# The first two tiles of an MLP: tile 1's first layer ahead of tile 0's second, both as seven products of quarters

## The chip, the cores and the metric

The kernel runs on one core of one Trainium2 chip. The metric is the device time of one execution in microseconds (us). A core has five engines that each work through their own list of instructions in order and wait for each other by semaphores: TensorE (PE in the profile; its weight loads are PEld), VectorE (DVE), ScalarE (ACT), GpSimd (POOL) and SyncE (SP). POOL and SP also issue the DMA transfers, POOL those that turn fp32 in memory into fp16 on the chip.

## The reference

An attention without softmax for 8 batches of 8 heads, 576 rows and a head width of 64, then an MLP over all 4608 rows:

```python
kv = np.einsum('bhsd,bhse->bhde', k, v)
out = np.einsum('bhsd,bhde->bhse', q, kv)
rms = np.sqrt(np.mean(out * out, axis=-1, keepdims=True) + 1e-06)
attn = out / rms * g_norm
x = attn.transpose(0, 2, 1, 3).reshape(4608, 512)
h = x @ w_in                       # 512 x 2048
g = h * (1.0 / (1.0 + np.exp(-1.702 * h)))
result = g @ w_out                 # 2048 x 512
```

## The kernel before

**Tiles.** There are nine tiles of 512 rows for the MLP: tile t < 8 holds the first 512 rows of batch t, tile 8 the last 64 rows (the `rest`) of all eight batches. Each tile has a first layer (x by w_in, gate, result gT) and a second (gT by w_out, result osb, stored to memory). A batch's attention has, for each of four pairs of heads: `q` (transposes on TensorE, copy qT on VectorE; batches 0 and 1 only), `kv` (products of k and v; copies to kvb or kvd), `out` (product with q; square on ScalarE), `ss` (sum of squares on TensorE; inverse root `rs` on ScalarE) and `apply` (VectorE writes x). From batch 2 on q is turned by DMA, the product comes out by rows (`rows`, `add_up`, `roots`, `turn`), and x is turned by DMA. Batch t+1's attention is spread over tile t.

**Products of quarters.** From tile 2 on a layer is not computed as 64 products of 512 columns but, after Strassen and Winograd, from quarters of its two matrices: seven products of quarters, 16 matrix products of 256 columns each, 112 in all. They need sums of quarters, which VectorE forms: of w_in (`w_in_sum`, ws), of w_out (`weight_sum`, tw), of x (`Sums`, xS) and of gT (`Seven.sums`, gS). In a first layer (`SevenIn`, L482) the columns are cut into four parts; a step such as "12" of a `Plan` is product 2 of part 1, four matrix products; banks of PSUM are copied in between and added (L480, L544, L546). In a second layer (`Seven`, L558) the products run in `ORDER`; `keep` copies a bank to SBUF on ScalarE, `place` adds or copies into osb. Tile 1 already runs its second layer so; both layers of tile 0 and tile 1's first are plain products (L422, L760).

**Order.** No scheduler moves anything: each engine runs its instructions as the Python code emits them. `dense` (L725) emits a tile; the dictionaries u1 and u2 hang other work behind a column, a step or a product: `at1(12, ...)` runs behind column 12 of the first layer, `at2(36, ...)` behind product 36 of the second. For tile 0 that is:

```python
at1(12, of(1, "pack_q", c))
at2(9 + 3 * c, of(1, "q", c))
at2((36, 37, 46, 47)[c], of(1, "kv", c))
o = (41, 43, 52, 53)[c]
at2(o, of(1, "out", c))
```

So batch 1's attention lies in tile 0's second layer. g_norm is multiplied into x for batch 0 (`apply` with g_col, L339); for the others w_in itself is scaled (`scale_w_in`, L188), in tile 0's second layer, ahead of the `w_in_sum`.

**Loads.** POOL issues one software queue in the order of the code: batch 0's q, k, v by pairs, w_in, then w_out's first quarter, batch 1's q, and so on alternately (L879 to L889). An issue waits for the landing of the one eight back. SP issues the stores and the DMA transposes, also in one order.

**Buffers.** PSUM has eight banks in three pools: ps_a (3), ps_h (3), ps_o (2). Of SBUF, gT and gS have one buffer each, osb and the copies of `keep` (qf) two.

Of the kernel before, what the change touches and what calls it, by code (L numbers as in the profile page):

```python
# [12 lines left out]
P = 128  # L13
# [3 lines left out]
def kernel(  # L17
# [27 lines left out]
    GROUP = 6  # L45
# [19 lines left out]
    qbuf = const.tile([P, NPAIR * NJ * P], F16)  # L65
    kraw = const.tile([P, NPAIR, 2 * NJ * D], F16)
# [121 lines left out]
    def scale_w_in(ko, engine):  # L188
        w = w_in_sb[:, ko]
# [5 lines left out]
    class Attention:  # L195
# [140 lines left out]
        def apply(self, c):  # L336
            o, rs, n = self.o[c]
            if c < NPAIR and self.b == 0:
# [12 lines left out]
    class Early(Attention):  # L351
        KEEP = 2
# [12 lines left out]
    class First(Early):  # L365


        ss_pool = (ps_o, "o")
# [23 lines left out]
    class Second(Early):  # L392


        ss_pool = rest_pool = (ps_h, "hT")

# [161 lines left out]
    class Seven:  # L558
# [10 lines left out]
        def sums(self, i0, i1, which=(0, 1, 2, 3)):  # L569
# [49 lines left out]
        def place(self, name, mo, with_, i, j):  # L619
# [9 lines left out]
            if self.t == B:  # L629
# [53 lines left out]
    def hid_seven(t, hid, seven, units1):  # L683
# [10 lines left out]
        for n, step in enumerate(todo.steps):  # L694
# [12 lines left out]
            for i0, i1, which in todo.ready.get(n, ()):  # L707
                seven.sums(i0, i1, (which,))
# [7 lines left out]

        left = {n: [lambda x=x: late(x) for x in steps] for n, steps in todo.late.items()}
        end = lambda: seven.sums(HF - 2, HF, (0,))
# [6 lines left out]
    def dense(t, units1, units2, group, deep, hid=None):  # L725
        hid = hid or Hidden(t)
        gT = hid.gT
        seven = None if deep else Seven(t, gT)
        cols = range(FO) if deep else [f for i in range(HF) for f in (i, HF + i)]
        ready = {} if deep else {8: (0, 4), 13: (4, 6), 15: (6, 8, (0,))}  # L730
        if group and t:
            order = [(ko, fo) for part in ((0, 3, 1, 2), range(4, group)) for ko in (0, 1) for fo in part]
            order += [(ko, fo) for ko in range(2, KO) for fo in range(group)]
            for ko, i in order:
                pool = (ps_h, "hT") if i < 3 else (ps_a, "att") if i == 3 else (ps_o, "o")
                hid.mm(ko, cols[i], *pool)
            for i in range(group):
                hid.gate(cols[i])
        left = {}
        if t >= SEVEN:  # L740
            left = hid_seven(t, hid, seven, units1)
            cols = ()
        for i, fo in enumerate(cols):
            if i >= group:
                for ko in range(KO):
                    hid.mm(ko, fo)
                hid.gate(fo)
            for u in units1.get(i, ()):
                u()
            if i in ready:  # L750
                seven.sums(*ready[i])
# [289 lines left out]
```

## Time and profile before

| what | us |
|---|---|
| median of three runs | 263.76 (263.72 to 264.36) |
| the profiled execution, time | 263.92 |
| the profiled execution, span of its instructions | 262.1 |
| TensorE, busy in the span | 253.6 |
| VectorE | 185.1 |
| ScalarE | 173.6 |
| GpSimd | 43.7 |

The span runs from the first to the last instruction of the core; all places in time below are counted from its start. The granted TensorE clock was 0.996 of full speed over the span. A row of the profile reads: line of the kernel, engine, operation, what it writes `<-` what it reads, shape, `x` count, then total busy time and the mean of one in ns, then the idle time of that engine just ahead of it and what ended it. In a view by time a row starts with its start and its length in us, and several equal instructions are merged into one. In the chain that ended last, a row is a piece of the one path from the end of the kernel back to its start. The rows of DMA issues give how many, the KB of each as they land, and the median time from issue to landing.

### The profile page before, as it was taken

To read this page: it belongs to the slowest core of one execution; us is meant where nothing else is said; L and a number is where in the kernel's file an instruction comes from. 1 tells how busy PE (TensorE), PEld (TensorE's weight loads), DVE (VectorE), ACT (ScalarE), POOL (GpSimd) and SP (SyncE) were. 2 spreads that over 40 slices of the span, in tenths; PEclk is the share of its full clock that TensorE was granted. 3 is DMA by queue.
4 is the path that set the end of the run, shared out by engine and by line. 5 is a ranking of instruction groups with operands and counts; after the bars stand their busy time and mean duration, and the time that the engine had idled before them with its cause. 6 is when DMAs were issued, how large, how long until landed. Compare 5 with 4: busy or idle time off the path is not lost.

```text
span 262.1 us, 6210 instructions
## 1 busy us (share of the span) xinstructions
PE 253.6 (97%) x2556; PEld 204.3 (78%) x2556; DVE 185.1 (71%) x324; ACT 173.6 (66%) x308; POOL 43.7 (17%) x68
## 2 busy tenths in 40 slices
PE   6899999999999999999999999999999999999992
PEld 5434554447888988898889988998899888888882
DVE  1540378868768995899589958995899587567831
ACT  3459836776649963996489748974798469737810
POOL 8863242005005001400050005000000000000000
PEclk9999999999999999999999999999999999999998
DMA  7999999999989946996899769946600620021005
GB/s 173 197 199 205 205 203 177 217 206 130 163 180 172 221 58 160 117 240 83 145 154 196 102 157 150 237 54 154 165 0 8 156 83 0 3 100 63 0 3 160
DMA packets 59806, 35.32 MB, mean 135 GB/s; under 512 B 31554, under 2 KB 57154, under 8 KB 59650
## 3 DMA queue, kind: packets, MB, share of 16 engines
q0 software_dynamic: 28608, 18.17, 50.1%
q1 hardware_dynamic: 30768, 16.36, 27.1%
q8 instruction: 20, 0.33, 0.5%
q10 hardware_dynamic: 402, 0.39, 0.5%
q14 instruction: 8, 0.07, 0.1%
HBM read 36.70 MB, written 9.44 MB: 176 GB/s over the span
## 4 chain that ended last, share of the span: by engine, by line
PE 92%; DMA 4%; POOL 1%; DVE 0%; issue 0%; ACT 0%; ACTq 0%
PE o L648 37%; PE h L530 33%; PE hT L422 10%; PE o L760 5%; PE kvp L221 2%; DMA vbuf<-in_v_dram 2%; DMA qraw<-in_q_dram 2%; PE outR L281 2%; PE ss L329 1%; PE outT L254 0%; PE q L403 0%; PE outT L258 0%; POOL kraw L89 0%; ACT sq L272 0%; DVE osb L628 0%
## 5 line engine op out<-in xcount | busy, mean ns | idle before, releaser
L648 PEld LDWEIGHTS <-gS 128*128 128x128 f16 x512 | 49.8, 98 | 5.5
L510 ACT ACTIVATE gT<-h 128x512 f16<-128x512 f32 x84 | 46.2, 605 | 5.1 <-PE h L530 5.1
L530 PEld LDWEIGHTS <-ws 128*128 128x128 f16 x448 | 43.8, 98 | 5.1
L648 PE MATMUL o<-tw,gS 128*128 128x256 f16 x384 | 46.3, 273 | 0.0
L530 PE MATMUL h<-xS,ws 128*128 128x256 f16 x336 | 45.3, 273 | 0.0
L648 PEld LDWEIGHTS <-gT 128*128 128x128 f16 x384 | 37.1, 98 | 4.2
L530 PEld LDWEIGHTS <-w_in_sb 128*128 128x128 f16 x336 | 32.5, 98 | 3.9
L648 PE MATMUL o<-w_out_sb,gT 128*128 128x256 f16 x256 | 33.3, 273 | 0.0
L422 PE MATMUL hT<-xT,w_in_sb 128*128 128x512 f16 x128 | 28.9, 379 | 0.0
L625 DVE TENSOR_TENSOR osb<-o,qf 128x512 f32<-128x512 f32 (+1 forms) x25 | 16.7, 668 | 15.6 <-PE o L648 12.8
L530 PE MATMUL h<-xT,w_in_sb 128*128 128x256 f16 x192 | 27.1, 273 | 0.0
L89 POOL DMA_DIRECT2D kraw<-in_k_dram x11 | 8.1, 733 | 106.3 <-PE kvp L221 87.8
L580 DVE TENSOR_TENSOR gS<-gT 128x512 f16<-128x512 f16 (+2 forms) x34 | 22.0, 653 | 4.5 <-ACT gT L431 3.9
L544 DVE TENSOR_TENSOR h<-h,s 128x512 f32<-128x512 f32 x28 | 19.5, 698 | 7.4 <-PE h L530 5.6
L422 PEld LDWEIGHTS <-w_in_sb 128*128 128x128 f16 x128 | 12.3, 98 | 15.4 <-issue 0.9
L431 ACT ACTIVATE gT<-hT 128x512 f16<-128x512 f32 x32 | 17.6, 613 | 7.0 <-PE hT L422 7.0
L546 DVE TENSOR_TENSOR s<-h,s 128x512 f32<-128x512 f32 x28 | 19.4, 692 | 4.0 <-PE h L530 3.3
L331 ACT ACTIVATE rs<-ss,eps_t 128x512 f32<-128x512 f32 (+1 forms) x16 | 9.2, 584 | 16.4 <-PE ss L329 16.3
L510 ACT ACTIVATE gT<-s 128x512 f16<-128x512 f32 x28 | 17.3, 628 | 1.2 <-DVE s L546 1.2
L944 ACT ACT_TABLE_LOAD x14 | 18.0, 1283 | 0.3
L681 POOL DMA_DIRECT2D out_dram<-osb x2 | 1.1, 562 | 94.1 <-DVE osb L625 94.1
L760 PE MATMUL o<-w_out_sb,gT 128*128 128x512 f16 x64 | 16.7, 380 | 0.0
(93 smaller groups left out, 367.6 us busy)
## 6 DMA issues: line engine op xcount, KB each, us to landing
out_dram<-osb SPq DMA_DIRECT2D x10, 512.0 KB, 3.5
kraw<-in_k_dram POOLq DMA_DIRECT2D x6, 576.0 KB, 8.7
vbuf<-in_v_dram POOLq DMA_DIRECT2D x6, 576.0 KB, 12.1
qraw<-in_q_dram POOLq DMA_DIRECT2D x3, 512.0 KB, 13.3
qbuf<-in_q_dram POOLq DMA_DIRECT2D x3, 512.0 KB, 14.0
out_dram<-osb SPq DMA_DIRECT2D x6, 192.0 KB, 6.9
w_in_sb<-in_moe_w_in_dram POOLq DMA_DIRECT2D x4, 256.0 KB, 7.5
w_out_sb<-in_moe_w_out_dram POOLq DMA_DIRECT2D x2, 512.0 KB, 14.0
```

The source lines that it names most:

```text
L331: nc.scalar.activation(rs[:, 0:n], t[:, 0:n], AFT.Abs_reciprocal_sqrt, bias=eps_t, scale=1.0 / D)
L422: nc.tensor.matmul(self.h[fo], w_in_sb[:, ko, fo * P : (fo + 1) * P], self.x[:, ko], start=(ko == 0), stop=(ko == KO - 1),)
L431: nc.scalar.activation(self.gT[:, fo, :], self.h[fo], AFT.Gelu_apprx_sigmoid)
L510: nc.scalar.activation(self.gT[:, to, n * TH : (n + 1) * TH], src, AFT.Gelu_apprx_sigmoid)
L530: nc.tensor.matmul(bank[name][:, a], w, x, start=(p in (1, 5) and a == 0 and k == 0), stop=(k == KH - 1), skip_group_check=True,)
L544: nc.vector.tensor_add(bank["z"], bank["x"], self.s5)
L546: nc.vector.tensor_add(self.s5, bank["x"], self.s5)
L580: op(s[:, n, lo], a, b)
L625: nc.vector.tensor_add(o, ps, self.kept[with_][:, m])
L648: nc.tensor.matmul(o, a, w, start=(p in (1, 2, 5) and i == 0 and (mo == 0 or split)), stop=(i == HF - 1), skip_group_check=True,)
L760: nc.tensor.matmul(os[mo], gT[:, fo, mo * P : (mo + 1) * P], w_out_sb[:, fo, :], start=(fo == 0), stop=(fo == FO - 1),)
L944: u2.setdefault(i, []).append(lambda: f(*args))
```

## The change

The start of the kernel is put in another order: tile 0's first layer (still plain products, by columns), tile 1's first layer, tile 0's second, tile 1's second. Tile 1's first and tile 0's second layer become seven products of quarters. gT gets two buffers, gS stays one that tiles 0 and 1 share, and osb and qf go from two buffers to one.

- Batch 1's attention moves from tile 0's second layer into columns 8 to 15 of its first. Its k-v are kept pair by pair (`KEEP` 1) in two small copies each. Since ScalarE has its inverse-root table loaded for it, columns 12 to 15 are not gated at once: VectorE copies them into osb (free until then), and `gate_held` gates them within tile 1's first layer.
- Batch 1's x is scaled by g in `apply`, as batch 0's is. So w_in is scaled only behind both first layers: the four parts of w_in on ScalarE in tile 0's second layer, the four sums ws on GpSimd.
- All of batch 1's q, k, v are loaded ahead of w_out, in eight pieces ("q02" is q of pairs 0 and 1).
- The second layers of tiles 0 and 1 run in the order `FIRST`, and each half of their osb is stored as soon as it is there, in four pieces.
- The 64 `rest` rows of batch 0 move from tile 0 to tile 7; their q is kept in q_rest.

```diff
-    GROUP = 6
+    GROUP, HELD = 6, 12
...
-    gpool = ctx.enter_context(tc.tile_pool(name="gpool", bufs=1))
+    gpool = ctx.enter_context(tc.tile_pool(name="gpool", bufs=2))
     spool = ctx.enter_context(tc.tile_pool(name="spool", bufs=1))
-    opool = ctx.enter_context(tc.tile_pool(name="opool", bufs=2))
+    opool = ctx.enter_context(tc.tile_pool(name="opool", bufs=1))
...
-            rows = stage.tile([P, 6, 2 * P], F32, name="qf", tag="qf", bufs=2)
+            pool, tag, n1 = (opool, "osb", 8) if n == "v" else (stage, "qf", 6)
+            rows = pool.tile([P, n1, 2 * P], F32, name=tag, tag=tag, bufs=1)
...
-                self.kvp = ps_a.tile([P, NPAIR, D], F32, name="kvp", tag="att")
+                pool, tag = (ps_o, "o") if self.b < EARLY and c > 1 else (ps_a, "att")
+                self.kvp = pool.tile([P, NPAIR, D], F32, name="kvp", tag=tag)
...
-            if c < NPAIR and self.b == 0:
+            if c < NPAIR and self.b < EARLY:
...
-        KEEP = 2
+        KEEP = 1
+        ss_pool = (ps_o, "o")
...
+        def keep_rest(self):
+            for c in range(NPAIR):
+                nc.vector.tensor_copy(q_rest[:, c], self.qT[c][:, SM:S])
+        def rest(self, c):
+            return q_rest[:, c]
...
-            x = x if t < B else x.rearrange("p c (j r) -> p c j r", j=J)
+            x = x if EARLY <= t < B else x.rearrange("p c (j r) -> p c j r", j=J)
...
+        FIRST = (1, 2, 6, 5, 7, 3, 4)
-        def __init__(self, t, gT):
+        def __init__(self, t, gT, s=None):
             self.t, self.gT = t, gT
-            self.s = spool.tile([P, 4, HF, 2 * P], F16, name="gS", tag="gS")
+            self.s = s or spool.tile([P, 4, HF, 2 * P], F16, name="gS", tag="gS")
...
-                k = stage.tile([P, 6, HN], F32, name="qf", tag="qf", bufs=2)
+                k = stage.tile([P, 6, HN], F32, name="qf", tag="qf", bufs=1)
...
+            elif self.t < EARLY and j == 1 - i:
+                store_early(self.t, 2 * i * P, (2 * i + 2) * P)
...
-            for p in self.LAST if self.t == B else self.ORDER:
+            for p in self.FIRST if self.t < EARLY else self.LAST if self.t == B else self.ORDER:
...
+    def first_columns(hid, units):
+        for i in range(GROUP, FO):
+            for ko in range(KO):
+                hid.mm(ko, i)
+                if ko == 1:
+                    for u in units.get(i - 0.5, ()):
+                        u()
+            if i < HELD:
+                hid.gate(i)
+            else:
+                nc.vector.tensor_copy(osbs[0][:, i - HELD, :], hid.h[i])
+            for u in units.get(i, ()):
                 u()
...
+    def gate_held(hid, i):
+        nc.scalar.activation(hid.gT[:, i, :], osbs[0][:, i - HELD, :], AFT.Gelu_apprx_sigmoid)
+    sevens = {}
+    def first_layer(t, units, s=None):
+        hid = Hidden(t)
+        sevens[t] = Seven(t, hid.gT, s)
+        return hid_seven(t, hid, sevens[t], units)
+    def second_layer(t, units, left, later):
+        if t:
+            osbs[t] = opool.tile([P, 4, DM], F32, name="osb", tag="osb")
+        seven = sevens[t]
+        todo = {n: [lambda x=x: seven.sums(*x) for x in xs] for n, xs in later.items()}
+        for n, us in units.items():
+            todo.setdefault(n, []).extend(us)
+        for n, us in left.items():
+            todo[n] = us + todo.get(n, [])
+        seven.run(todo)
+        if EARLY <= t < B and t not in HALVED:
+            store(t, 0, J)
...
-    load_w_out(0, 4)
-    early_load("q", 1, 0, NPAIR)
-    load_w_out(4, 8)
-    early_load("k", 1, 0, 2)
-    load_w_out(8, 10)
-    load_w_out(10, 12)
-    early_load("v", 1, 0, 2)
-    early_load("k", 1, 2, NPAIR)
-    early_load("v", 1, 2, NPAIR)
-    load_w_out(12, 14)
-    load_w_out(14, FO)
+    for n, c0, c1 in ("q02", "k02", "v02", "q24", "k23", "v23", "k34", "v34"):
+        early_load(n, 1, int(c0), int(c1))
+    for f in range(0, FO, 4):
+        load_w_out(f, f + 4)
...
+    SECOND = Plan(
+        "11 01 21 12 05 15 06 22 16 25 03 02 07 26"
+        " 17 31 35 04 23 13 36 27 14 32 37 24 33 34",
+        {},
+        {},
+        {1: 'ADAA', 5: 'ADAD'},
+        "A",
+        "aaoa",
+        "aohh",
+        {},
+        (2, 4, 3, 4),
+    )
...
+    osbs[0] = opool.tile([P, 4, DM], F32, name="osb", tag="osb")
+    sevens[0] = Seven(0, d0.gT)
+    u, at = hooks()
+    at(6, a0.keep_rest)
+    for l in range(2):
+        at(6, nc.vector.memset, kvd[l], 0.0)
+    at(7, start, 1)
+    at(7, w_in_sum, 0)
+    for c in (0, 1):
+        at(8, of(1, "pack_q", c))
+        at(9 + c, of(1, "q", c))
+        at(11, of(1, "kv", c))
+        at(12, of(1, "out", c))
+        at(13, of(1, "ss", c))
+    at(10, w_in_sum, 2)
+    at(11, w_in_sum, 1)
+    at(11, table, ROOT)
+    for c in (2, 3):
+        at(12, of(1, "pack_q", c))
+        at(13, of(1, "q", c))
+    at(13, w_in_sum, 3)
+    for c in (0, 1):
+        at(13, of(1, "apply", c))
+    at(13, of(1, "kv", 2))
+    at(14, of(1, "kv", 3))
+    at(14, of(1, "out", 2))
+    at(14.5, of(1, "out", 3))
+    at(15, of(1, "ss", 2))
+    at(15, of(1, "apply", 2))
+    first_columns(d0, u)
...
+    u, at = hooks()
+    at(0, of(1, "ss", 3))
+    at(0, of(1, "apply", 3))
+    at(0, table, GELU)
+    at(1, load_q, 2)
+    at(1, load_kv, 2)
+    begin(at, 1, 2)
+    for i, n in enumerate((4, 8, 15, 21)):
+        at(n, gate_held, d0, HELD + i)
+    at(16, sevens[0].sums, 0, 4, 0, 1)
+    at(27, weight_sum, 0)
+    left = first_layer(1, u, sevens[0].s)
+    u, at = hooks()
+    at(0, weight_sum, 1)
+    for n, ko in ((16, 0), (48, 1), (64, 2), (82, 3)):
+        at(n, scale, w_in_sb[:, ko], nc.scalar)
+    for n in range(2):
+        at(2, scale, ws[:, n].rearrange("p k f -> p (k f)"), nc.gpsimd)
+    at(33, weight_sum, 2)
+    at(35, weight_sum, 3)
+    at(72, of(2, "kv_all", "D"))
+    ask(at, 78, 3)
+    for n in range(2, 4):
+        at(80, scale, ws[:, n].rearrange("p k f -> p (k f)"), nc.gpsimd)
+    at(82, sevens[1].sums, 0, 8, 0)
+    at(86, sevens[1].sums, 0, 8, 1)
+    second_layer(0, u, {}, {1: ((4, 8, 0, 1),), 34: ((0, 8, 2, 3),)})
+    u, at = hooks()
+    attend(at, 2, LATER.attn)
+    begin(at, 100, 3)
+    second_layer(1, u, left, {20: ((0, 8, 2),), 58: ((0, 8, 3),)})
...
+            for r, n in ((0, 16), (1, 36)):
+                at(n, setattr, live[r], "ss_pool", (ps_a, "att"))
+                at(n, of(r, "out", NPAIR))
+                at(n + 14, of(r, "ss", NPAIR))
+                at(n + 18, of(r, "apply", NPAIR))
+            at(26, table, ROOT)
+            at(56, table, GELU)
```

Below this the loop over the tiles 2 to 8 hangs the same work at the same places as before. `attend`, `ask` and `begin` gather calls that stood in the loop: batch t+1's attention, the loads of a batch, and the start of a batch with its DMA transposes.

More of the change, by code (lines that the diff above doesn't have):

```diff
@@ new lines, in hooks, with of, table, attend @@
+    def hooks():
+        units = {}
+        return units, lambda n, f, *args: units.setdefault(n, []).append(lambda: f(*args))
+    def of(b, name, *args):
+        return lambda: getattr(live[b], name)(*args)
+    def table(name):
+        nc.scalar.preload_act_table_set(name)
+    ROOT, GELU = "abs_reciprocal_sqrt_and_small", "gelu_apprx_sigmoid_and_others"
+    def attend(at2, b, at):
+        at2(at["table"], table, ROOT)
+        for h in range(2):
+            at2(at["roots"][h], of(b, "roots", h))
+        for j in range(J):
+            for name in ("rows", "add_up", "turn"):
+                at2(at[name][j], of(b, name, j))
+        at2(46, of(b, "out", NPAIR))
+        at2(74, of(b, "ss", NPAIR))
+        at2(80, of(b, "apply", NPAIR))
+        at2(82, table, GELU)
@@ new lines @@
+    at(33, weight_sum, 2)
[11 more added lines that the diff above has]
+    second_layer(1, u, left, {20: ((0, 8, 2),), 58: ((0, 8, 3),)})
+    for t in range(EARLY, NT):
+        b = t + 1
+        todo = plan(t)
+        u, at = hooks()
+        if b < B:
+            at(todo.steps.index("kv"), of(b, "kv_all", todo.keep))
+        if t + 2 < B:
+            ask(at, 15, t + 2)
+        left = first_layer(t, u)
+        u, at = hooks()
+        if b < B:
+            attend(at, b, todo.attn)
+        elif t < B:
+            for r, n in ((0, 16), (1, 36)):
[5 more added lines that the diff above has]
+            at(56, table, GELU)
+        if t + 2 < B:
+            begin(at, 100, t + 2)
+        second_layer(t, u, left, todo.later)
```

178 lines of the change are left out of this document (22 added, 156 removed).

## The prediction

> **What bounds the kernel now.** I read the page's busy shares first, then the chain that ended last in order of time.
>
> ```profile
> PE 253.6 (97%) x2556; PEld 204.3 (78%) x2556; DVE 185.1 (71%) x324; ACT 173.6 (66%) x308; POOL 43.7 (17%) x68
> 22.06 6.91 PE hT L422 x32
> 31.24 0.26 PE q L403 x6
> 34.21 3.89 PE o L760 x18
> 38.10 0.31 PE kvp L221 x12
> 40.01 0.22 PE outT L254
> 41.30 0.22 PE ss L329
> 208.24 10.92 PE h L530 x100
> ```
>
> TensorE is busy 97% of the span, and from 22 us on the chain consists of its products, one behind the other: nothing else is waited for. So the time is the sum of TensorE's work, and any wait that the change puts in front of TensorE is paid in full, because later stages have no slack to give it back. The rows price a product: 512 columns 6.91/32 = 0.216 us (also 3.89/18), 256 columns 10.92/100 = 0.109 us; a pair's six transposes 0.26, its twelve k-v products 0.31, `out` and `ss` 0.22 each.
>
> The loads of the start run in one software queue, in issue order, and fill it:
>
> ```profile
> 24.53 0.67 POOL L89 DMA_DIRECT2D kraw<-in_k_dram  x1 [1.23 <-DMA w_in_sb<-in_moe_w_in_dram]
> 27.07 0.67 POOL L89 DMA_DIRECT2D vbuf<-in_v_dram  x1 [1.87 <-DMA w_out_sb<-in_moe_w_out_dram]
> 29.76 0.71 POOL L180 DMA_DIRECT2D w_out_sb<-in_moe_w_out_dram  x1 [2.02 <-DMA qraw<-in_q_dram]
> 29.50 1.39 DVE L96 COPY qbuf<-qraw 96x768 f16<-96x768 f16 x4 [10.49 <-DMA qraw<-in_q_dram]
> w_out_sb<-in_moe_w_out_dram POOLq DMA_DIRECT2D x2, 512.0 KB, 14.0
> qraw<-in_q_dram POOLq DMA_DIRECT2D x1, 576.0 KB, 14.1
> kraw<-in_k_dram POOLq DMA_DIRECT2D x2, 288.0 KB, 15.0
> ```
>
> POOL, waiting for landings, goes on at 24.53 (the last of w_in), 27.07 (the first 512 KB of w_out) and 29.76 (batch 1's q, 576 KB): 1088 KB in 5.23 us, 208 KB/us. Batch 1's q is first used at 29.50, in tile 0's second layer, where 64 products wait for nothing of it.
>
> **What the change takes away.** Two layers of 64 products of 512 columns become 112 of 256: 64 x 0.216 - 112 x 0.109 = 13.8 - 12.2 = 1.6 us each, **-3.2 us** for both. Batch 0's remainder (`out`, `ss`) only moves to tile 7. The first layers of tile 1 and of tile 0 now stand before any second layer, so batch 1's whole attention has to be done within tile 0's last eight columns.
>
> **The stretch from 22 to 42 us.** TensorE's own work from column 8 (at 22.0) to the first product of tile 1 that needs all of x, step "12": eight columns 6.9, transposes 1.0, k-v 1.2, four `out` and four `ss` 1.7, three products 1.3: 12.2 us, so 34.2 without a wait. Against this stands VectorE, which now holds one after the other:
>
> ```profile
> L409 DVE COPY qT<-q 128x576 f16<-128x576 f16 x4 | 1.8, 455 | 1.1 <-PE q L403 1.1
> L448 DVE TENSOR_TENSOR ws<-w_in_sb 128x2048 f16<-128x2048 f16 x2 | 2.4, 1220 | 0.0
> L769 DVE COPY osb<-o 128x512 f32<-128x512 f32 x2 | 1.4, 679 | 0.0
> L339 DVE SCALAR_TENSOR_TENSOR xT<-outT,g_col,rs 128x512 f16<-128x512 f32 x4 | 3.0, 744 | 1.7 <-ACT rs L331 1.7
> L357 DVE CAST kvb<-kvp 64x128 f16<-64x128 f32 x4 | 1.2, 288 | 1.3 <-PE kvp L221 1.3
> L842 DVE COPY g_col<-g_ps 128x1 f32<-128x1 f32 x1 | 0.1, 148 | 0.0
> L331 ACT ACTIVATE rs<-ss,eps_t 128x512 f32<-128x512 f32 x8 | 5.4, 694 | 2.9 <-PE ss L329 2.9
> 48.38 1.21 DVE L556 TENSOR_TENSOR tw<-w_out_sb,tw 128x2048 f16<-128x2048 f16 x1
> 49.51 1.22 DVE L556 TENSOR_TENSOR tw<-w_out_sb 128x2048 f16<-128x2048 f16 x1
> ```
>
> The last two rows start 1.13 us apart with 1.21 us each: an instruction behind another costs 0.08 less than its duration, so I take 1.14 for a weight sum, 0.38 for a qT copy, 0.6 for a held column, 0.66 for an `apply`; 0.35 for a pack (1.39/4). The copy of 64x64 is not in the trace: between 0.148 (one column) and 0.288 (128), I take 0.22. There are eight, since batch 1's k-v are now kept pair by pair.
>
> q02 (288 KB) lands 512 + 288 KB before the 29.50 of now: 29.50 - 800/208 = 25.65; then k02 at 27.0, v02 28.4, q24 29.8, k23 and v23 31.2, the last at 32.6.
> - Column 9 ends at 23.7; `q(0)` needs the pack of q02: 25.65 + 0.45. TensorE waits 2.4 us.
> - Column 10 and `q(1)` end at 27.5. From 27.7 VectorE runs the qT copy 0.38, `w_in_sum(2)` 1.14, four k-v copies 0.88, `w_in_sum(1)` 1.14, a held column 0.6, two packs 0.7, a held column 0.6: to 33.1. Meanwhile k-v waits 0.2 for v02, `q(2)` 0.4 for its pack; `q(3)` takes the PSUM bank of `q(2)` and waits 1.1 for its copy.
> - The copy of `q(3)` starts at 34.1 (0.38); `w_in_sum(3)` 1.14, two `apply` 1.3, two k-v copies 0.44: `out(2)` may start at 37.4, while TensorE has been ready since 35.4. A held column and two copies more: `out(3)` at 38.4.
> - Column 15 ends at 39.1, `ss(2)` 0.22, its root 0.69, `apply(2)`, the copy of a product, `apply(3)` 0.74: step "12" at 42.3.
>
> 42.3 - 34.2 = **+8.1 us**. The bounds: with 0.15 a copy and 0.35 for the first pack 7.3; with 0.29 a copy and 0.08 more on each of the 15 long ones 9.9.
>
> **Between the layers.**
>
> ```profile
> L648 PE MATMUL o<-tw,gS 128*128 128x256 f16 x384 | 46.3, 273 | 0.0
> L628 ACT COPY osb<-o 128x512 f32<-128x512 f32 x7 | 4.1, 586 | 18.3 <-PE o L648 18.3
> 50.80 4.05 ACT L431 ACTIVATE gT<-hT 128x512 f16<-128x512 f32 x8 [1.57 <-PE hT L422]
> 31.29 3.88 ACT L191 ACTIVATE w_in_sb<-w_in_sb,g_col 128x2048 f16<-128x2048 f16 x2
> ```
>
> Tile 1's second layer now follows tile 0's at once. Its first product writes the bank that ScalarE still copies out (the last product 0.27, the copy 0.59): +0.9; two more bank waits of 0.1. ScalarE has 25 copies and gates in tile 1's first layer, the four held columns among them: 8 gates in a row took 4.05, so 12.7 us beside 12.2 of TensorE; it starts late and ends in the second layer, whose banks it doesn't hold: nothing, up to +1 where it does. Scaling w_in on ScalarE (four of 2 us) lies in tile 0's second layer, 13.1 us long with four copies of 0.6. Total **+1.1**.
>
> **One output buffer.** osb has one buffer instead of two, and tile 1's first `place` comes 31 products into its layer. VectorE waits there until tile 0's eight stores have landed, with the four `turn`, tile 1's last sum (0,8,3) and so product 3 queued behind it.
>
> ```profile
> L625 DVE TENSOR_TENSOR osb<-o,qf 128x512 f32<-128x512 f32 x23 | 15.8, 689 | 15.0 <-PE o L648 12.4 <-issue 2.6
> 45.29 4.53 SPq L795 DMA_DIRECT2D out_dram<-osb  x8
> out_dram<-osb SPq DMA_DIRECT2D x10, 512.0 KB, 3.5
> out_dram<-osb SPq DMA_DIRECT2D x6, 192.0 KB, 6.9
> out_dram<-osb SPq DMA_DIRECT2D x10, 64.0 KB, 4.4
> 68.23 2.48 DVE L309 TENSOR_TENSOR x<-outR,sum 128x512 f16<-128x512 f32 x4 [0.75 <-ACT sum L305]
> 77.31 1.72 DVE L480 CAST kvd<-kvp 64x256 f16<-64x256 f32 x4
> L580 DVE TENSOR_TENSOR gS<-gT 128x2048 f16<-128x2048 f16 x7 | 8.5, 1215 | 0.0
> ```
>
> Count from T, the end of tile 0's second layer. The k-v products of batch 2 end at T - 4.2; VectorE then has four casts 1.7, a `place` 0.6, two sums 2.4, and places product 3 until T + 1.2. Eight issues take 4.5: the last starts at T + 5.2. Landing took 3.5 (whole halves, quiet queue) to 6.9 us (these pieces, beside loads; here too batch 3 is being loaded): T + 8.7 to T + 12.1. Then `place` 0.7, four `turn` 2.5, the sum 1.2: T + 13.1 to 16.5. TensorE gets to product 3 at T + 0.9 + 80 x 0.109 + 1.1 = T + 10.7. So +2.4 to +5.8; the pieces are those of the second kind, half of them the small ones (4.4): I take **+4.0**.
>
> **Costed at nothing.** w_out comes behind all of batch 1: 2048 KB from 32.6 on land by 42.5, and its first reader, `weight_sum(0)`, stands at the end of tile 1's first layer, about 52; without these ten us tile 0's second layer would wait. Batch 2's loads follow it as they do now. The scalings of ws on GpSimd must end before tile 2's products 5, 14 us and more away. The `rest` of batch 0 adds an `out` and an `ss` of small products in tile 7, taken from tile 0. The second halves of tiles 0 and 1 are stored by the same eight pieces.
>
> **Sum**, against the profiled execution's 263.92 us (0.16 above the median of 263.76): -3.2 + 8.1 + 1.1 + 4.0 = +10.0: **273.9 us**.
>
> **Rivals.**
>
> *GpSimd's scaling holds VectorE up.* Four scalings of ws, 2048 columns each, go to GpSimd, whose only work of this kind was:
>
> ```profile
> 1.02 0.29 POOL L139 TENSOR_SCALAR_AFFINE_SELECT ident<-ident 128x128 f16<-128x128 f16 x1 [0.56 <-DVE ident L137]
> 1.25 0.20 POOL L148 MEMSET ones<- 128x128 f16 x1
> 1.51 0.15 POOL L149 MEMSET ones<- 64x64 f16 x1
> ```
>
> 0.05 us for 64 columns more gives 1.8 us for 2048; 0.29 for 128 gives 4.6. The first two can start when the last parts' products 5 and 6 have read ws, steps 17 and 21 of 28, so some 4.8 us (11 x 4 x 0.109) before the end of tile 1's first layer, where VectorE's sums gS and tw stand in front of additions that TensorE needs. If a VectorE instruction with two SBUF inputs can't run beside them, that is 2 x 1.8 to 2 x 4.6 less the 0.8 of slack there, +2.8 to +8.4, and about +1 where the other two meet the sums before tile 0's stores: at 2.5 us each some 279. No row of before has GpSimd and VectorE computing together, so the trace is neutral. [...]
>
> *The stores don't hold it.* Landing in 3.5 us or less, and VectorE at the short end of its bounds: -3.2 + 7.3 + 1.1 + 1.0 = 270. For it: later tiles' halves land in 3.5; against: batch 3's loads start at product 78.
>
> *Not slower.* VectorE instructions that stand one behind the other may overlap further than the 0.08 us of the two weight sums, since these are its longest. Of the waits between 23.7 and 42.3 only the first, 2.4 for q02, is set by the queue; the other 5.7 are VectorE's, with 28 instructions behind the first pack. At 0.2 less for each they are gone. The same saving on the 8 instructions ahead of tile 0's first store (1.6) and on the six behind the landing (1.2) takes the buffer's wait from 2.4, with the shorter landing, to nothing: -3.2 + 2.4 + 1.1 = +0.3: 264.2. It decides from 0.2 us an instruction on. Against it:
>
> ```profile
> L309 DVE TENSOR_TENSOR x<-outR,sum 128x512 f16<-128x512 f32 x24 | 14.9, 683 | 0.8 <-ACT sum L305 0.8
> ```
>
> Four `turn` of 0.683 took 2.48 in a row, again 0.08 less for each that follows.
>
> **Chances.** Forecast 0.50 (own range 271 to 276.5), GpSimd 0.33, stores quiet 0.12, not slower 0.05. The range reaches from the quiet case with half a microsecond less at several places, 268.5, into the GpSimd case up to 281. Changes within 0.3% (0.8 us) can't be told from none here. The last rival's 0.05 is split, faster 0.02 (were more saved than it says) and the same 0.03; slower 0.95.
>
> **What would show it.** TensorE idle from 23.7 to about 26, before `outT` near 37 and before step "12" near 42, each released by VectorE; tile 0's second layer beginning near 53; 112 products in each of the four layers; VectorE idle on out_dram stores in tile 1's second layer, with TensorE waiting before product 3. [...] I am wrong if TensorE stays dense from 22 to 42, or if the first products of tile 2 begin before 80 us.

## The result, and the profile after

The changed kernel takes 286.36 us (median of 4 runs, 285.32 to 288.65) beside 263.78 us (263.72 to 264.36) of the kernel before on the same chip: a ratio of 1.086, 95% interval 1.079 to 1.093. The forecast was 273.9, its range ended at 281: the sign was right, the size was 12.5 us short.

Where the time went is read from busy times by stage. First two stretches of the kernel before, up to the first product of tile 2 and behind it (columns: stretch and its length, then busy time and instructions of each engine, the granted TensorE clock, DMA):

```profile
22.00:75.46 53.46, 53.46 (x427) 31.34 (x423) 34.05 (x58) 35.08 (x56) 11.18 (x15) 1.00 1.20 187
75.46:262.10 186.64, 181.91 (x1918) 162.69 (x1916) 142.83 (x246) 127.38 (x236) 15.82 (x22) 0.99 0.62 113
```

The busy shares on the page of the kernel after, and then its stages: to 42.30, where the prediction had the first product that needs all of tile 1's x, the rest of tile 1's first layer, tile 0's second layer, tile 1's second layer, and all that follows.

```profile
PE 258.6 (91%) x2652; PEld 216.2 (76%) x2652; DVE 214.1 (75%) x348; ACT 180.6 (63%) x317; POOL 65.5 (23%) x73
```

```profile
22.00:42.30 20.30, 14.68 (x122) 6.97 (x121) 14.39 (x29) 9.91 (x17) 7.95 (x11) 0.92 1.28 204
42.30:58.60 16.30, 13.38 (x107) 10.94 (x106) 14.76 (x19) 13.21 (x25) 9.07 (x2) 0.90 1.02 144
58.60:72.00 13.40, 13.40 (x160) 11.65 (x159) 13.20 (x15) 9.96 (x9) 5.89 (x7) 0.99 0.21 27
72.00:98.30 26.30, 16.97 (x136) 13.60 (x135) 20.11 (x18) 8.43 (x14) 10.51 (x2) 0.81 0.65 117
98.30:284.90 186.60, 182.20 (x1924) 162.91 (x1921) 143.23 (x246) 128.11 (x238) 15.87 (x22) 1.00 0.65 114
```

TensorE, busy 97% before, is at 91%, and GpSimd has 22 us more to do. Behind tile 2's first product both kernels need 186.6 us. All of the loss, 98.30 - 75.46 = 22.8 us, lies ahead of it. There TensorE is busy for 58.4 of 76.3 us: it idles 17.9 us where it idled none before. And its clock is 0.81 to 0.92 in three of the four stages, a term that the prediction does not have. TensorE's waits in that stretch (in all, times, longest):

```profile
PE o L654 <- ACT qf L621: 5.9, 1, 5.9
PE h L533 <- DVE h L547: 2.8, 1, 2.8
PE o L654 <- DVE gS L584: 2.7, 1, 2.7
PE q L406 <- DVE qbuf L97: 2.3, 2, 1.9
PE outT L257 <- DVE kvb L361: 2.0, 2, 1.8
PE q L406 <- DVE qT L412: 0.8, 1, 0.8
PE o L654 <- ACT osb L632: 0.7, 1, 0.7
PE h L533 <- DVE xT L342: 0.3, 1, 0.3
```

The lines 4, 5, 6 and 8 are the stretch from 22 to 42 us, foreseen step by step; the seventh is the bank wait between the layers. The third is the wait ahead of product 3 that one output buffer was to cost (forecast 4.0). The first two, 8.7 us, have no place in the sum. The group of the scalings (busy time, mean ns), and GpSimd's and VectorE's rows of the timeline around those waits (start, duration):

```profile
L195 POOL TENSOR_SCALAR ws<-ws,g_col 128x2048 f16<-128x2048 f16 x4 | 21.8, 5447 | 12.2 <-DVE s L549 12.2
```

```profile
49.52 10.88 POOL L195 TENSOR_SCALAR ws<-ws,g_col 128x2048 f16<-128x2048 f16 x2 [12.18 <-DVE s L549]
71.61 10.89 POOL L195 TENSOR_SCALAR ws<-ws,g_col 128x2048 f16<-128x2048 f16 x2
...
50.02 3.76 DVE L584 TENSOR_TENSOR gS<-gT 128x1024 f16<-128x1024 f16 x1
56.66 3.09 DVE L559 TENSOR_TENSOR tw<-w_out_sb 128x2048 f16<-128x2048 f16 x1
70.00 6.44 DVE L584 TENSOR_TENSOR gS<-gT 128x2048 f16<-128x2048 f16 x1
76.48 5.39 DVE L584 TENSOR_TENSOR gS<-gS,gT 128x2048 f16<-128x2048 f16 x1
88.78 0.69 DVE L629 TENSOR_TENSOR osb<-o,qf 128x512 f32<-128x512 f32 x1 [2.80 <-DMA out_dram<-osb]
```

A scaling takes 5.45 us. Beside it a sum of 128x1024 takes 3.76 instead of 0.69 and sums of 128x2048 take 3.09, 6.44 and 5.39 instead of 1.22: VectorE is held for 3.1 + 1.9 + 5.2 + 4.2 = 14.3 us. At 88.78 tile 1's first `place` then waits 2.8 us more for tile 0's stores.

The longest wait of TensorE, from 77.27 to 83.21, has two parts, which its weight load and ScalarE's copy tell apart:

```profile
81.92 0.10 PEld L654 LDWEIGHTS <-gS 128*128 128x128 f16 x1 [4.93 <-DVE gS L584]
82.58 0.58 ACT L621 COPY qf<-o 128x512 f32<-128x512 f32 x1 [7.64 <-DVE osb L629]
```

Some 4.6 us pass until the second held sum is there. The last 1.3 go to the one buffer of qf: ScalarE's copy into it, which frees TensorE's bank, waits for VectorE's last `place` of tile 0 (81.79), which stands behind the held sums. The prediction has no price for qf's second buffer, and no run gives it back, so this share of 1.3 us is read from the rows alone.

The clock is seen best in windows of 3.41 us, laid where the granted clock changes:

```profile
34.89:38.30 3.41, 1.41 (x17) 0.48 (x15) 3.35 (x8) 0.55 (x1) 1.55 (x2) 1.00 1.24 206
38.30:41.71 3.41, 3.17 (x9) 1.35 (x10) 1.40 (x3) 1.49 (x4) 0.00 (x0) 0.50 1.24 205
51.95:55.37 3.42, 0.63 (x6) 0.42 (x5) 3.38 (x4) 0.71 (x2) 3.41 (x2) 1.00 0.90 142
55.37:58.78 3.41, 3.41 (x18) 2.36 (x17) 3.06 (x3) 3.04 (x7) 3.41 (x1) 0.50 0.00 0
75.85:79.26 3.41, 1.42 (x13) 1.02 (x11) 3.38 (x2) 0.00 (x0) 3.41 (x2) 1.00 1.48 188
79.26:82.67 3.41, 0.00 (x0) 0.10 (x1) 3.41 (x3) 0.09 (x1) 3.25 (x1) 0.50 0.11 8
82.67:86.09 3.42, 2.88 (x14) 2.02 (x14) 3.30 (x5) 2.75 (x5) 0.00 (x0) 0.50 0.65 173
89.50:92.91 3.41, 0.83 (x7) 0.48 (x5) 3.41 (x6) 1.76 (x2) 0.00 (x0) 1.00 0.31 58
92.91:96.33 3.42, 3.28 (x16) 2.37 (x17) 1.01 (x3) 0.00 (x0) 0.00 (x0) 0.50 0.54 100
```

Each window in which TensorE was busy for 1.42 us or less is followed by one at clock 0.50. In the slow window from 55.37 four products of 256 columns take 0.85 us, 0.213 each, where they take 0.109 at full clock. TensorE was busy for 12.7 us in the five slow ones; by an estimate from these two figures about half of it, 6.4 us, was lost. The account of the 22.8 us: 17.9 idle, 6.4 clock, -3.2 for fewer products, and 1.7 left, which is about what the eleven waits cost beyond themselves, by an estimate: a product of 256 columns alone takes 0.273, in a row 0.109, so 0.16 more at each restart.

### The profile page after: what moved, and what is told of

It is laid out like the page before. It is cut to its first block, busy times and chain, and to the rows that moved or that the text cites. A ratio compares the mean times of both kernels' runs of the same rounds, so it can differ in the third digit from the quotient of the medians.

```text
span 284.9 us, 6451 instructions
## 1 busy us (share of the span) xinstructions
PE 258.6 (91%) x2652; PEld 216.2 (76%) x2652; DVE 214.1 (75%) x348; ACT 180.6 (63%) x317; POOL 65.5 (23%) x73
## 4 chain that ended last, share of the span: by engine, by line
PE 73%; DVE 13%; DMA 7%; POOL 2%; issue 2%; SPq 1%; ACT 0%; DVEq 0%
PE o L654 35%; PE h L533 33%; DVE gS L584 6%; DMA w_in_sb<-in_moe_w_in_dram 4%; DMA qraw<-in_q_dram 2%; PE kvp L224 2%; PE outR L284 2%; POOL w_in_sb L155 1%; DVE ws L451 1%; SPq L776 1%; DMA out_dram<-osb 1%; DVE x L312 1%; DVE xT L342 1%; DVE osb L629 1%; DVE osb L745 1%
## 5 line engine op out<-in xcount | busy, mean ns | idle before, releaser
L654 PEld LDWEIGHTS <-gS 128*128 128x128 f16 x576 | 57.2, 100 | 16.9 <-DVE gS L584 7.9
L654 PE MATMUL o<-tw,gS 128*128 128x256 f16 x432 | 53.1, 277 | 5.9 <-ACT qf L621 5.9
L513 ACT ACTIVATE gT<-h 128x512 f16<-128x512 f32 x96 | 52.8, 604 | 5.0 <-PE h L533 4.9
L533 PE MATMUL h<-xS,ws 128*128 128x256 f16 x384 | 51.9, 273 | 2.8 <-DVE h L547 2.8
L533 PEld LDWEIGHTS <-w_in_sb 128*128 128x128 f16 x384 | 37.8, 99 | 6.6 <-issue 1.6
L584 DVE TENSOR_TENSOR gS<-gT 128x512 f16<-128x512 f16 (+2 forms) x33 | 32.3, 984 | 0.7 <-ACT gT L513 0.7
L195 POOL TENSOR_SCALAR ws<-ws,g_col 128x2048 f16<-128x2048 f16 x4 | 21.8, 5447 | 12.2 <-DVE s L549 12.2
L621 ACT COPY qf<-o 128x512 f32<-128x512 f32 (+1 forms) x29 | 16.0, 553 | 12.6 <-DVE osb L629 7.6
L654 PE MATMUL o<-w_out_sb,gS 128*128 128x256 f16 x144 | 18.8, 288 | 2.7 <-DVE gS L584 2.7
L533 PE MATMUL h<-xS,w_in_sb 128*128 128x256 f16 x128 | 19.8, 282 | 0.0
## 6 DMA issues: line engine op xcount, KB each, us to landing
vbuf<-in_v_dram POOLq DMA_DIRECT2D x6, 576.0 KB, 12.7
```

The costliest lines, as they stand in the source:

```text
L195: engine.tensor_scalar_mul(w, w, g_col)
L513: nc.scalar.activation(self.gT[:, to, n * TH : (n + 1) * TH], src, AFT.Gelu_apprx_sigmoid)
L533: nc.tensor.matmul(bank[name][:, a], w, x, start=(p in (1, 5) and a == 0 and k == 0), stop=(k == KH - 1), skip_group_check=True,)
L584: op(s[:, n, lo], a, b)
L621: nc.scalar.copy(self.kept[as_][:, m], ps)
L654: nc.tensor.matmul(o, a, w, start=(p in (1, 2, 5) and i == 0 and (mo == 0 or split)), stop=(i == HF - 1), skip_group_check=True,)
```

## The experiments

**GpSimd's scaling.** On VectorE in place of GpSimd, and then, in the same two places, on ScalarE:

```diff
-        at(2, scale, ws[:, n].rearrange("p k f -> p (k f)"), nc.gpsimd)
+        at(2, scale, ws[:, n].rearrange("p k f -> p (k f)"), nc.vector)
...
-        at(80, scale, ws[:, n].rearrange("p k f -> p (k f)"), nc.gpsimd)
+        at(80, scale, ws[:, n].rearrange("p k f -> p (k f)"), nc.vector)
```

> The four scalings of ws stand on VectorE instead of GpSimd, nothing else is changed. Theory (GpSimd's 5.45 us scalings shut out VectorE's additions with two SBUF inputs, and the TensorE waits behind them halve the clock): the gS and tw rows go back to 0.69 and 1.22 us, each scaling costs VectorE at most 1.2 us, and the time falls by 9 to 15 us, to 271 to 277, of which 4 to 6 us are clock; the granted clock between 42 and 98 us rises from 0.90 to above 0.96. The window of half clock near 38.4 us stays, since its wait lies ahead of any scaling. Rival (the sums were late by themselves, in a VectorE that is full there): four more instructions on VectorE, so 286 or more and gS sums still ending at the same places. Rival (one osb buffer is the main loss): the wait for out_dram stores grows from 2.8 us to over 8 and the time stays above 280.

```diff
-nc.gpsimd)
+nc.scalar)
```

> The four scalings of ws stand on ScalarE. Theory: as with VectorE, gS and tw at 0.69 and 1.22 us; a scaling is 2.0 us on ScalarE (as its rows for w_in_sb), two of them stand ahead of the copies that free tile 0's first banks, so up to 2 us are given back: 272 to 279. If ScalarE's scaling held VectorE's two-input additions up as GpSimd's does, these would again be 2 us longer each, and the time some 280.

On VectorE 280.66 us (279.39 to 282.54), on ScalarE 281.85 (279.96 to 284.06). In both every gS is back at 0.69 or 1.22 us and the wait of 2.8 us in tile 1's first layer is gone, so the long rows came from GpSimd's scalings, and ScalarE's do not cause them. But the gain is 5.7 and 4.5 us where 9 to 15 and 7 to 14 were expected, and on VectorE the clock from 42 to 98 us is 0.92, not above 0.96. The rows of VectorE's kernel say why: its first `place` of tile 1 comes early and now waits 6.09 us for the stores instead of 2.80. This is the second rival of that run in part: the time stays above 280, though the wait does not reach 8 us.

```profile
59.59 1.41 DVE L195 TENSOR_SCALAR ws<-ws,g_col 128x2048 f16<-128x2048 f16 x2
82.43 0.69 DVE L629 TENSOR_TENSOR osb<-o,qf 128x512 f32<-128x512 f32 x1 [6.09 <-DMA out_dram<-osb]
```

On ScalarE two scalings of 2.01 us also stand ahead of the copies that free tile 0's first banks (a wait of 2.9 us behind `qf`).

**GpSimd's scalings by themselves.** The kernel before, with four such multiplications of a scratch tile that nothing reads, in tile 3's first layer:

```diff
+                if t == 3:
+                    for _ in range(4):
+                        at1(late, nc.gpsimd.tensor_scalar_mul, scratch, scratch, g_col)
```

> The kernel before, with four multiplications of 128x2048 f16 of a scratch tile by g on GpSimd in tile 3's first layer. Nothing reads the scratch. Theory (an exclusive lock for the length of the GpSimd instruction, against VectorE instructions with two SBUF inputs alone): each scaling takes 5.3 to 5.6 us; each gS and xS row that falls beside one ends at least 3 us late, up to 22 us of GpSimd in all; additions, copies and reduces that read PSUM keep their 0.68 us. The time grows by 3 to 15 us, and the clock falls to half somewhere behind the waits. Rival (bandwidth shared): all VectorE rows beside a scaling are longer by the same share, and none by more than twice. Rival (the long gS rows came from something else): gS rows stay at 0.69 and 1.2 us and the time at 264.

274.65 us in one run, 10.6 more. The timeline of this kernel: GpSimd's row, and some of VectorE's beside it.

```profile
108.06 22.08 POOL L943 TENSOR_SCALAR scratch<-scratch,g_col 128x2048 f16<-128x2048 f16 x4
...
108.31 3.74 DVE L464 TENSOR_TENSOR xS<-xT,xS 128x512 f16<-128x512 f16 x1
116.30 0.70 DVE L546 TENSOR_TENSOR h<-h,s 128x512 f32<-128x512 f32 x1 [0.22 <-PE h L532]
119.99 3.92 DVE L582 TENSOR_TENSOR gS<-gT 128x2048 f16<-128x2048 f16 x1
124.87 4.08 DVE L582 TENSOR_TENSOR gS<-gS,gT 128x1024 f16<-128x1024 f16 x1
```

Instructions with two inputs in SBUF are held in this run: `xS` takes 3.74 us instead of 0.42, `gS` 3.92 instead of 1.22 and 4.08 instead of 0.69. An addition with an input in PSUM, in the middle of a scaling, takes its 0.70. Less its own length, each held instruction ends 1.9 us before GpSimd's row does: if the hold starts with the row, and if the row's ends are exact, it lasts by this estimate some 3.6 us of the 5.45 that one takes here too. VectorE was held 9.7 us in all, TensorE waited 6.7, and two windows of half clock follow (from 112.85 and 129.92). The theory had VectorE shut out for the whole length of a scaling; that was not shown, since the rows have it free again 1.9 us before the end.

**One output buffer.** The scalings on VectorE, and 4 KB a partition for the first half of tile 1's osb (paid for with one of three buffers of `rs`):

```diff
+    osb_low = const.tile([P, 2, DM], F32)
...
-            o = osbs[self.t][:, 2 * i + m.start : 2 * i + m.stop, j * HN : (j + 1) * HN]
+            osb = osb_low if (self.t, i) == (1, 0) else osbs[self.t]
+            o = osb[:, 2 * i + m.start : 2 * i + m.stop, j * HN : (j + 1) * HN]
```

> The scalings on VectorE, and tile 1's first half of osb in a buffer of its own (4 KB a partition), so that its first place does not wait for tile 0's stores; rs has two buffers instead of three. Theory: the 4.0 us that the prediction gave the one buffer are there, so 3 to 5 us faster than the kernel with the scalings on VectorE alone, 267 to 273, and no wait of VectorE for out_dram stores before tile 2. Rival (the stores do not hold it): within 1 us of that kernel.

271.97 us (271.13 to 272.21): 8.7 less than with one buffer, about twice what was expected. In the one-buffer kernel TensorE waits twice there, 5.4 us in all, as the prediction's upper end had it:

```profile
83.17 0.27 PE L332 MATMUL ss<-sq,ones 128*128 128x256 f16 x1 [2.69 <-DVE osb L629]
86.70 3.60 PE L654 MATMUL o<-w_out_sb,gS 128*128 128x256 f16 x16 [2.71 <-DVE gS L584]
```

The other 3.3 may be the two windows of half clock behind it. To split them, the one-buffer kernel again, with 40 products by a zero weight where TensorE waits:

```diff
+    def idle(n):
+        bank = sevens[1].banks("x", 1)
+        for _ in range(n):
+            nc.tensor.matmul(
+                bank, zero, w_out_sb[:, 0, 0:HN], start=False, stop=False, skip_group_check=True
+            )
+
+    at(73, idle, 20)
+    at(77, idle, 20)
```

> The kernel with the scalings on VectorE and one osb buffer, with 40 products by a zero weight, added to the bank of product 7 of tile 1's second layer: 20 ahead of ss, where TensorE waits 2.7 us, 20 ahead of product 3, where it waits 2.7 us again. The sums are unchanged. Theory (a stretch of 3.41 us in which TensorE was busy for less than about 42% is followed by a stretch at half clock, 1.7 us of work lost each): VectorE's wait for tile 0's stores stays at 6 us, the two stretches of half clock behind it (85 to 92 us) go, and the time falls by 2.5 to 4 us, to 276.5 to 278. Rival (the clock falls with the time that products wait for operands, whatever TensorE does meanwhile): the stretches stay and the time is 280 to 282.

276.99 us (276.33 to 278.04). Windows of the one-buffer kernel at the wait (two lines), then of this one:

```profile
81.90:85.32 3.42, 0.81 (x6) 0.48 (x5) 2.89 (x5) 1.76 (x2) 0.00 (x0) 1.00 0.00 0
85.32:88.73 3.41, 2.03 (x10) 1.48 (x11) 2.25 (x4) 0.00 (x0) 0.00 (x0) 0.50 0.82 154
```

```profile
81.52:84.94 3.42, 2.61 (x25) 2.30 (x24) 3.31 (x6) 1.76 (x2) 0.00 (x0) 1.00 0.05 12
84.94:88.35 3.41, 2.88 (x27) 2.34 (x26) 2.33 (x4) 0.00 (x0) 0.00 (x0) 1.00 0.79 147
```

Work that computes nothing makes the kernel 3.7 us faster: VectorE waits there for 6.40 us, not less than the 6.09 before, and the half clock is gone. So the price of an idle stretch is shown, and apart from the stretch itself; the 5.0 us left to the kernel at 271.97 are about the two waits.

**Do the two add?** The scalings back on GpSimd, tile 1's own half of osb kept:

```diff
-        at(2, scale, ws[:, n].rearrange("p k f -> p (k f)"), nc.vector)
+        at(2, scale, ws[:, n].rearrange("p k f -> p (k f)"), nc.gpsimd)
...
-        at(80, scale, ws[:, n].rearrange("p k f -> p (k f)"), nc.vector)
+        at(80, scale, ws[:, n].rearrange("p k f -> p (k f)"), nc.gpsimd)
```

> The changed kernel with the scalings on GpSimd as they were, and tile 1's own half of osb. Theory (GpSimd's lock and the one buffer delay the same VectorE queue one behind the other, so that part of the lock's delay is hidden in the wait for the stores: that wait was 2.8 us with the lock and 6.1 without it): the lock alone costs 5.7 + 3.3 = 9 us, so 279 to 283, and the buffer only 4 to 6 us on top of it. Rival (two separate costs that add): 272.0 + 5.7 = 277.7, 277 to 278.5.

283.26 us (282.49 to 283.44), just above the theory's 279 to 283 and far from the sum of two separate costs. So the scalings on GpSimd, which the theory calls the lock, cost 5.7 us with one buffer and 11.3 without; the buffer costs 3.1 beside them (4 to 6 expected) and 8.7 without. Both delay the same VectorE queue, and whichever comes second finds it late already.

**The stretch from 22 to 42 us.** On top of the kernel at 271.97, w_in_sum by columns:

```diff
-    at(7, w_in_sum, 0)
+    for i in range(4):
+        at(7, w_in_sum, i, 0, 5)
...
+    for n, i in ((4, 0), (6, 1), (8, 2), (10, 3)):
+        at(n, w_in_sum, i, 5, 8)
```

> On top of the kernel with scalings on VectorE and tile 1's own half of osb: w_in_sum is cut by columns. Columns 0 to 4 of all four sums run while VectorE waits for q02 (22 to 25 us), columns 5 to 7 in tile 1's first layer behind apply(3). Theory (VectorE's chain sets the waits between 27 and 42 us): the three sums that stood behind the first pack, 3.4 us, are off the chain; the waits before q(3), out(2), out(3) and step 12, 3.8 us in the kernel it is built on, shrink to under 1 us, the wait for q02 (2 us) stays, and the time falls by 2 to 4 us, to 268 to 270. Rival (the loads set the stretch): it falls by less than 1 us.

270.55 us (268.96 to 272.44): 1.4 less, with q02's wait of 2.1 us still there and the others at 2.4 instead of 4.2. The waits shrink as the theory has it, the time by less than it expected, and the runs of this kernel differ by more than the gain. Then q02, k02 and v02 ahead of w_in's last columns (the same run moves columns 2 to 4 of the sums behind the packs), and after that the held columns on ScalarE:

```diff
-    load_w_in(13, FO)
...
         early_load(n, 1, int(c0), int(c1))
+        if n + c0 == "v0":
+            load_w_in(13, FO)
```

> On top of that, q02, k02 and v02 are loaded ahead of the last three columns of w_in, and columns 2 to 4 of the sums stand behind the packs. Theory (the wait for q02 is the queue's order: 768 KB at 205 KB per us stand ahead of it): q02 lands 3.7 us earlier and q(0)'s wait of 2 us goes; 1.5 to 2.5 us faster than with the sums alone, 266 to 268. Rival (the wait only moves to column 13, whose weights now land near 28 us): within 0.7 us.

```diff
-                nc.vector.tensor_copy(osbs[0][:, i - HELD, :], hid.h[i])
+                nc.scalar.copy(osbs[0][:, i - HELD, :], hid.h[i])
```

> On top of the load order, the four held columns are copied by ScalarE, which is idle from 33 to 38 us there, not by VectorE. Theory: up to 1 us faster where VectorE is still late for the second pair of heads, else no difference; 265 to 268. Rival: the copies stand in front of ScalarE's squares and roots and the time is up to 1 us longer.

268.18 (267.60 to 269.92) and 268.06 (267.63 to 268.55). q(0)'s wait is gone, so it was the order of the queue; the held copies make no difference. A last step put columns 14 and 15 behind all of batch 1:

```diff
         if n + c0 == "v0":
-            load_w_in(13, FO)
+            load_w_in(13, 14)
+    load_w_in(14, 15)
+    load_w_in(15, FO)
...
-    at(14, of(1, "kv", 3))
-    at(14, of(1, "out", 2))
-    at(14.5, of(1, "out", 3))
-    at(15, of(1, "ss", 2))
+    at(13, of(1, "kv", 3))
+    at(13, of(1, "out", 2))
+    at(13, of(1, "out", 3))
+    at(14, of(1, "ss", 2))
+    at(14, of(1, "ss", 3))
...
-            self.banks("z", 0)
+            if self.t != 1:
+                self.banks("z", 0)
```

> On top of the kernel with the new load order (without the held copies on ScalarE for columns 14 and 15): the loads of w_in's last three columns come one by one, columns 14 and 15 behind all of batch 1, and the second pair of heads is done ahead of column 14, so that its roots fall beside columns 14 and 15; tile 1's second layer takes the bank of product 3 first. Theory (what is left in the stretch is the landing of v23 and v34 and the chain from out(2) to apply(2)): the waits for k-v (0.8 us) and before step 01 (1.3 us) fall to under 0.8 us together and the bank wait of 0.7 us goes; 266 to 267.2. Rival (the wait moves to columns 14 and 15, whose weights land near 33 and 34 us): 267.5 to 269.

267.76 us (three runs from 267.22 to 268.26, one at 275.48): not told apart from the two before. Its waits in the stretch are 0.4 before k-v, 0.6 before `q`, 0.9 before `out` and 0.8 before a product, 2.7 us in all where the kernel it is built on had 2.9, and the bank wait of 0.7 is still there; columns 14 and 15 wait for nothing, so that neither theory nor rival held. All four steps together are worth some 4 us of the stretch's 8.

**The products of quarters.** One layer alone, tile 1's first, in the order of the kernel before:

```diff
-    SEVEN = 2
+    SEVEN = 1
+    ONE = Plan(
+        "11 01 21 12 05 22 15 06 16 25 03 02 07 kv 26 17 31 35 04 13 23 36 27 14 32 37 24 34 33",
...
-            x = x if t < B else x.rearrange("p c (j r) -> p c j r", j=J)
+            x = x if EARLY <= t < B else x.rearrange("p c (j r) -> p c j r", j=J)
```

> One part of the change alone, in the order of the kernel before: only tile 1's first layer is computed as products of quarters (112 of 256 columns instead of 64 of 512); tile 0's second layer stays dense and in its place, batch 1's attention stays within it, w_in is scaled where it was, both osb buffers stay. ws's last sum moves ahead of that layer, three sums of w_out into it and behind it. Theory (TensorE's 1.6 us are to be had only where VectorE has room: in that layer it now has four xS, eight additions, the sums gS and one tw, some 14 us by their rows, beside 12.2 us of TensorE): the layer's products are there but TensorE waits for VectorE at two or three places, 0.5 to 1.3 us each; 263.5 to 266. Rival (TensorE is the bound and the products count in full): 262 to 262.8, faster than before.

269.69 us (269.36 to 271.35): neither. Batch 2's k-v products stood at step 13, where TensorE waited 2.4 us for their v, with half clock behind it. They were moved eleven steps back:

```diff
-        "11 01 21 12 05 22 15 06 16 25 03 02 07 kv 26 17 31 35 04 13 23 36 27 14 32 37 24 34 33",
+        "11 01 21 12 05 22 15 06 16 25 03 02 07 26 17 31 35 04 13 23 36 27 14 32 kv 37 24 34 33",
...
-                at2(2, weight_sum, 2)
+                at1(18, weight_sum, 2)
```

> The same single layer in the order of the kernel before, with batch 2's k-v products eleven steps later (their v landed at 56.5 us, and TensorE stood in front of them for 2.4 us), the second sum of w_out in the first layer, and the sums gS for product 6 earlier. Theory: the wait for v (2.4 us) and the stretch of half clock behind it (1.7 us) go, so about 4 us less than the run before, 264 to 266; what is left of TensorE's waits (1.5 to 2 us) is VectorE's and takes the 1.6 us of fewer products up, so not faster than the kernel before by more than 0.3%. Rival (VectorE has room once the order is right): 262 to 263, faster than both kernels.

276.94 us: a miss of the experiment. Batch 3's k and v were loaded ahead of these products, which so computed batch 2 from batch 3's data, after a wait of 8.9 us; nothing follows for the theory. With those loads behind them:

```diff
-            late = 15 if todo else 11
+            late = 25 if t == 1 else 15
```

> The single layer of quarters once more, as in the run before, with batch 3's k, v and q asked for behind batch 2's k-v products; in the run before they were asked for ahead of these, so that batch 2's k-v products waited 8.9 us for batch 3's k and v and were made of them. Theory: neither wait nor stretch of half clock at the k-v products; TensorE waits 1.5 to 2 us for VectorE in all, which takes up the 1.6 us of fewer products: 264 to 266, not faster than the kernel before by more than 0.3%. Rival (VectorE has room once the order is right): 262 to 263, faster than both kernels.

265.87 us (median of 10 runs, 265.22 to 267.33), a ratio of 1.0067 (1.0046 to 1.0088). No k-v wait and no half clock in these layers; TensorE's waits there are now:

```profile
PE o L648 <- DVE osb L625: 0.4, 1, 0.4
PE o L648 <- DVE gS L580: 0.4, 1, 0.4
PE h L530 <- DVE s L546: 0.3, 1, 0.3
PE outR L281 <- ACT gT L510: 0.3, 1, 0.3
PE h L530 <- DVE h L544: 0.2, 1, 0.2
PE outR L281 <- ACT kvd L480: 0.2, 1, 0.2
```

Six waits of 1.8 us in all by VectorE and ScalarE, with a restart of 0.16 behind each, are more than the 1.6 us of products saved, as the theory had it; some 0.6 us of the 1.85 that this kernel is slower stay unexplained. Where it is lost was not expected: the layer of quarters itself runs from 47.48 to 62.12, 14.6 us beside 14.8 before, and the second layer behind it takes 15.3 us, where it took 13.3 and waited for nothing. None of the versions beats the kernel before.

## Why the prediction was wrong

- **The stretch from 22 to 42 us, +8.1: the mechanism right, the size partly by luck.** The first product that needs all of x came at 43.1 (forecast 42.3). But 1.6 us of it are the window of half clock from 38.30, and TensorE's waits there add up to 5.6 us, not 8.1: waits forecast too long made up for the clock and the restarts, which the sum does not have. q02's wait was the queue's and most of the others VectorE's, as the loads and the sums by columns showed.
- **Fewer products, -3.2: right in TensorE's work, as far as the account shows; open as a gain.** Alone, one layer's 1.6 us are taken up by the waits for VectorE and ScalarE; tile 0's second layer was not tried alone.
- **Between the layers, +1.1: too high.** One wait of 0.7 us is there, the two of 0.1 are not seen.
- **One output buffer, +4.0: the mechanism right, the size at the upper end.** With the scalings on VectorE the wait is 5.4 us (forecast 2.4 to 5.8) and its clock 3.3 more. In the changed kernel it costs only 3.1, since the scalings on GpSimd had made VectorE late already. The rival that the stores do not hold it fell.
- **GpSimd's scaling: this is the step that failed.** The sum puts the four scalings at nothing, under "Costed at nothing", and VectorE's two sums gS ahead of tile 0's stores at 2.4 us. The runs showed 11.8 us for these two, and 5.7 us of the time for the scalings on GpSimd beside the one buffer, 11.3 without it. That they hold VectorE up was a rival with a chance of 0.33; its mechanism came true, its figure of some 279 did not. Its price was wrong in two places. The scaling was taken at 2.5 us, between 1.8 and 4.6; it takes 5.45, past the bound from the 128-column row. And the second pair was priced at "about +1 where the other two meet the sums": product 80 starts it, products 82 and 86 queue the sums gS behind it, so these met it for their whole length, 9.4 us of VectorE and 5.9 of TensorE (1.3 of them through qf). No row of before had such an instruction; of the two that gave the bounds, the slow one reads its tile as the scaling does, the fast one only writes, and a figure nearer the fast one was taken all the same.
- **The clock: a term that is not in the sum.** 6.4 us here. Before, the clock was 0.996 over the span, and from 22 us on TensorE waited for nothing; the prediction put 13 us of waits into the kernel and kept that clock. In the changed kernel every window of 3.41 us with TensorE busy for 1.42 us or less was followed by one at 0.50, so these waits cost more than their length.
- **Not slower** fell: TensorE's waits for VectorE from 27 us on did not go, though 3.5 us came where 5.7 were forecast, and sums gS one behind the other (64.08 and 65.22) save 0.08 us again.

## What to carry to other kernels

A new wait of TensorE had three prices here: the wait, a restart of some 0.16 us, and, by an estimate, up to 1.7 us for each window of 3.4 us at half clock, which here followed windows with TensorE busy for less than some 45%. Where a wait cannot go, products that compute nothing can be cheaper than idling; here they saved 3.7 us. Before an elementwise step goes to GpSimd, look for VectorE instructions with two SBUF inputs beside it: here they stood for some 3.6 of the 5.45 us of a multiplication of 128x2048. Two delays in one in-order queue need not add, so undo each of them with and without the other before a cost is given to either.

## What the runs showed of the hardware

- **The windows of half clock lay on one grid in each run.** In six profiled kernels the slow windows start whole multiples of 3.413 us apart (in the changed kernel at 38.30, 55.37, 79.26, 82.67 and 92.91); against the start of the span the grid stood at 0.2 to 3.4 us. At full clock, windows of large products with TensorE busy up to 43% were followed by half clock, those from 47% on by full clock, and at 44% to 46% both occurred (44.6% and 46.3% with half clock behind them, 44.3% and 45.3% with full); one window of 52 small products at the start, busy for 67%, was followed by half clock too. From half clock it returned after windows of 79% busy and more, and stayed after 59% and 71%. That the same waits cost differently from run to run was the author's estimate, not shown by itself: the changed kernel's four runs have mean clocks of 0.963 to 0.981 and spread over 3.3 us, those of before over 0.6.
- **GpSimd's 128x2048 multiplication by a column took 5.45 us**, VectorE's 0.75 and ScalarE's 2.01.
- **Not explained:** gS at 70.00 in the changed kernel was held although the scaling's row starts at 71.61, after gS would have ended, and so was gS at 71.32 (6.46 us, row at 72.94) in the run with the scalings on GpSimd and two buffers. GpSimd was issuing loads then, but these alone do not hold it: with the scalings on ScalarE, gS at 69.42 took its 1.21 us beside the same issues.
